# 64-column rows and 64x128 tiles for the turned sums of w, 40 weight columns for the turned state

## The chip, the cores and the metric

The kernel runs on one core of a Trainium2 chip. Its time is the device time of one execution in microseconds (us). Engines are named as in the profile: PE is TensorE's matmul, PEld its weight load, DVE is VectorE, ACT is ScalarE, POOL is GpSimd, and SP issues the DMAs.

## The reference

A recurrent attention layer (RWKV-7) over 4 batches, 8 heads, 768 positions and 40 columns a head, all FP32, and a two-layer network with exact GELU on its output:

```python
for t in range(S):
    y[:, :, t] = np.einsum('bhd,bhde->bhe', rt, state)
    Sa = np.einsum('bhde,bhe->bhd', state, at)
    state_decay = state * wt[:, :, None, :] - np.einsum('bhd,bhe->bhde', Sa, bt)
    state = state_decay + np.einsum('bhd,bhe->bhde', vt, kt)
...
x = attn_out.transpose(0, 2, 1, 3).reshape(B * S, H * D)     # 3072 x 320
h = x @ w_in                                                 # 320 x 2048
g = 0.5 * h * (1.0 + erf(h / sqrt(2)))
return g @ w_out                                             # 2048 x 320
```

## The kernel before

The 768 positions are cut into 12 chunks of 64 (`C`). Within a chunk the recurrence is turned into matrix products: with the running products of w (as exponentials of running sums of its logarithms) taken into a, r, b and k, a chunk needs products of 64x64, one inverse of a triangular matrix for each batch and head, and the state from the chunk before. The 128 partitions hold two halves of 64 (`half(0)`, `half(1)`); a head's 40 columns or rows stand in 64 places of a half.

Each piece of the work is a step, a generator named by its kind and its chunk (`w0` loads w of chunk 0, `sums0` sums its logarithms). A list written out by hand, `ORDER`, says in which order the steps go on; a number behind a colon names the pair of PSUM banks (`duo`) that a piece takes. Every engine carries out its instructions in the order in which the list issues them, and waits only for the data it needs. All loads of a step go into SP's queue, except stored inverses, which POOL issues. The list opens with `tails0 gaps1 w0 pads3 consts0 w1 pads2 zeros1 inv1 b0 a0 logs0 begin6`, and goes on to `sums0:0 sums0:1 v0 k0 logs1 sums0 wi0 consts0 sums1:2 sums1:3 pads0 ta0:1 sums0 pads1 sc0 sums1 ta0 tb0:0`. The change leaves it as it is.

The steps that matter here:

- `w` loads w of a chunk with positions on partitions. Chunks 0 and 2 go into `w_tile`, chunk 1 into the tile `SM`, which later holds masked sums; a row of a batch has its 8 heads side by side, 40 columns each. Behind the last head lie 24 columns (`REST`), zeroed by POOL in `tails`, since a matmul that takes 64 columns from the last head's start reads them.
- `logs` takes the logarithm in place (ACT, line 514).
- `sums` of the first three chunks has two parts. First the turned sums: for each head and each half of the positions one matmul with 64 columns of w's logarithms as weights (the head's 40 and 24 of the next one) and a triangular matrix of ones, `cum_m`, as the moving side; the running sums come out with a head's columns on partitions. Then the straight sums: one matmul for each batch pair with `cum_m` as weights and 320 moving columns. ACT takes the exponentials: those of the straight sums in place of w (line 537), the turned ones into `wpT` (line 540).
- `sc` (DVE, line 613) and `sk` (POOL, line 621) multiply b and k by the straight exponentials. In chunks 0 and 1 the products go into slices of the tile `extra`, called `padded`: slice `c % 2` for b, slice `2 + c % 2` for k. There each head has 64 columns, of which `pads` zeroes the last 24 (POOL, line 377); the list issues `pads3` and `pads2` near its start.
- `ta`, `tb`, `tk` turn a, b and k (PE, line 572); `N`, `A`, `RV` are products of 64x64; `sq`, `cornerd`, `joinedd` invert chunk 0's matrix on PE, `inv` the other chunks' on POOL (lines 819 and 821), through DRAM (`nb`, `ft`).
- `tn` turns the state for the products with r: 40 rows of `st` as weights, an identity of 40 columns as moving side. For chunks 1 and 2 it works on full 128 rows; from chunk 3 on there are 32 matmuls a chunk, each with 64 weight columns (the 40 of the state and the 24 next to them). ACT copies the result to the tile `turned` (line 1009), whose rows of each half up to 40 `yy` then uses as weights.
- `ph`, `pc`, `pd`, `pg`, `po` are the two-layer network (lines 1191 to 1347), which fills PE between the pieces of the recurrence.

One FP32 matmul stands in the trace as two records of PE and two of PEld. Most small matmuls go through the helper `mm` and so have its line, 154; they are told apart by their tiles and shapes, such as `64*128 64x128`: 64 rows and 128 columns of weights, then rows and columns of the moving side.

Of the kernel before, what the change touches and what calls it, by code (L numbers as in the profile page):

```python
# [13 lines left out]
ACT = mybir.ActivationFunctionType  # L14
# [83 lines left out]
def kernel(  # L98
# [15 lines left out]
    nc = tc.nc  # L114
    B, H, S, D = r.shape
    DM, DF = moe_w_in.shape
    P = 128
    C = 64
    HP = 64
    BL = 32  # L120
    NP = H // 2
    NA = H // 4
    G = B // 2
# [6 lines left out]
    REST = HP - D  # L130
# [7 lines left out]
    def sb(name, shape, dtype=FP32):  # L138
        return const.tile(shape, dtype, name=name)
# [4 lines left out]
    def duo():  # L144
        return duos[places.pop(0)]

    def half(j, n=HP):
        return slice(j * HP, j * HP + n)
# [4 lines left out]
    def mm(o, lhsT, rhs, first=True):  # L153
        nc.tensor.matmul(o, lhsT, rhs, start=first, stop=True, skip_group_check=True)  # L154
# [3 lines left out]
    NT, NB, NW, NS = FIRST  # L158
# [4 lines left out]
    w_tile = sb("w_tile", [P, G * DM + REST])  # L163
# [5 lines left out]
    b_rows, k_rows = ([t[:, n * RW:(n + 1) * RW] for t in two_rows] for n in range(2))  # L169
    st = sb("st", [P, 2, NP, G, VC])  # L170
    SM = sb("SM", [P, 2, G, NP, VC])
# [7 lines left out]
    TW = 2 * G * NP * D  # L179
    turned = sb("turned", [P, LW])  # L180
# [13 lines left out]
    def plain(t):  # L194
        return t.rearrange(" ".join(["p"] + list("abcd")[:len(t.shape) - 1]) + " -> p (" + " ".join("abcd"[:len(t.shape) - 1]) + ")") \
            if len(t.shape) > 2 else t

    padded = extra.rearrange("p (n g h d) -> p n g h d", n=4, g=G, h=H)
# [11 lines left out]
    raws, queue = {}, [nc.sync]  # L210

    def rows(t):
        return t[:, :G * DM].rearrange("p (g h d) -> p g h d", g=G, h=H)

    def rows_of(src, c, e):
        return src[G * e:G * (e + 1), :, c * C:(c + 1) * C, :].rearrange("g h t d -> t (g h) d")
# [4 lines left out]
    def load(out, in_):  # L221
        queue[0].dma_start(out=out, in_=in_)  # L222

    def fetch(c, n, src, t):
        for e in range(2):
            load(t[half(e)].rearrange("p g h d -> p (g h) d")[:, :, :D], rows_of(src, c, e))
        raws[c, n] = t
# [17 lines left out]

    @step
    def w_(c):
        t = plain(SM)[:, :G * DM + REST] if c == 1 else w_tile
        to = rows(t)
        if c < NB:  # L250
            fetch(c, "w", w, to)
            raws[c, "w"] = t
            yield
        else:
            for e in range(2):
                for g in range(G):
                    load(to[half(e ^ g), g], w[G * e + g, :, c * C:(c + 1) * C].rearrange("h t d -> t h d"))
                raws[c, "w"] = t
                yield
# [59 lines left out]
    ident = sb("ident", [P, P])  # L319
    cum_m = sb("cum_m", [P, P])  # L320
# [7 lines left out]

    @step
    def tails(c):  # L330
        for t in (w_tile, plain(SM)) if c == 0 else (b_rows[0], k_rows[0]):
            nc.gpsimd.memset(t[:, G * DM:G * DM + REST], 0.0)
        yield

# [173 lines left out]
    def of(c):  # L508
        return this.setdefault(c, {})

    @step
    def logs(c):
        logw = raws[c, "w"][:, :G * DM]
        nc.scalar.activation(logw, logw, ACT.Ln)
        yield

    @step
    def sums(c):
        t, logw = of(c), raws.pop((c, "w"))
        wp = t["wp"] = wps[c % 2]  # L520
        if c < NW:
            pt = duo().rearrange("p e (n t) -> p e n t", t=C)
            for n in range(G * NP):
                for x in range(2):
                    for e in range(2):
                        at = (2 * n + x) * D
                        mm(pt[half(x), e, n], logw[half(e), at:at + HP], cum_m[half(e), half(e)])
            yield
        cum = duo()[:, :, :DM]
        for g in range(G):  # L530
            for e in range(1 if c < NB else 2):
                q = half(e ^ g) if c >= NB else slice(0, P)
                mm(cum[half(e) if c >= NB else q, g], cum_m[q, q], logw[q, g * DM:(g + 1) * DM])
        yield
        rw = logw[:, :G * DM].rearrange("p (g m) -> p g m", g=G)
        t["rw"] = rows(logw)
        nc.scalar.activation(rw, cum, ACT.Exp, scale=-1.0)  # L537
        yield
        if c < NB:
            nc.scalar.activation(wp[:, :, 1:].rearrange("p (n e) t -> p e n t", e=2), pt, ACT.Exp)  # L540
            yield
        elif c < NW:
            en = t["en"] = by_batch(kT_tile)
            for to, scale_ in ((wp[:, :, 1:].rearrange("p (g n e) t -> p g e n t", g=G, e=2), 1.0),
                               (en.rearrange("p (e g n) t -> p g e n t", e=2, g=G), -1.0)):
                for g in range(G):
                    nc.scalar.activation(to[:, g], pt[:, ::1 - 2 * g, g * NP:(g + 1) * NP], ACT.Exp, scale=scale_)
            yield
# [37 lines left out]
    def by_batch(t):  # L586
        return t.rearrange("p g n t -> p (g n t)").rearrange("p (n t) -> p n t", t=C)
# [402 lines left out]
    @step  # L990
    def tn(c):
        if c < NB:
            pt = duo()[:, :, :NP * BW].rearrange("p e (n t) -> p e n t", n=NP)
            for e in range(2):
                for i in range(NP):
                    for g in range(G):
                        mm(pt[half(g), e, i], st[:, e, i, g, :HP], ident.rearrange("p (x d) -> p x d", x=2)[:, :, :D])
            yield
            nc.scalar.copy(turned[:, :TW].rearrange("p (e n) -> p e n", e=2), pt.rearrange("p e n t -> p e (n t)"))
            yield  # L1000
            return
        pt = duo()[:, :, :G * NP * D].rearrange("p x (n d) -> p x n d", d=D)
        for e in range(2):
            for i in range(NP):
                for g in range(G):
                    for x in range(2):
                        mm(pt[half(g), x, e * NP + i], st[half(x, D), e, i, g, :HP], ident[half(x, D), half(x, D)])
        yield
        nc.scalar.copy(turned[:, :TW].rearrange("p (n x d) -> p x n d", x=2, d=D), pt)
        yield  # L1010

    def sums_of_y(c):
# [424 lines left out]
```

## Time and profile before

| What | us |
|---|---|
| median of 3 runs | 660.76 |
| lowest and highest run | 656.54, 661.46 |
| span of the profiled execution, first to last instruction | 653.2 |
| PE busy | 633.2 (97%) |
| PEld busy | 573.0 (88%) |
| DVE, ACT, POOL busy | 483.1, 274.7, 387.0 |

The profile page gives no time of its own for the profiled execution but its span; the time of a run holds what lies around the span too, 3.3 us by the lowest run and 8.3 us by the highest. The share of busy time is an average over stages: the first 130 us load the weights and bring the first chunks in, with DMA near its limit, and the last 100 us have little but the network left.

### The profile page before, as it was taken

To read this page: it belongs to the slowest core of one execution; us is meant where nothing else is said; L and a number is where in the kernel's file an instruction comes from. 1 tells how busy PE (TensorE), PEld (TensorE's weight loads), DVE (VectorE), ACT (ScalarE), POOL (GpSimd) and SP (SyncE) were. 2 spreads that over 40 slices of the span, in tenths; PEclk is the share of its full clock that TensorE was granted. 3 is DMA by queue.
4 is the path that set the end of the run, shared out by engine and by line. 5 is a ranking of instruction groups with operands and counts; after the bars stand their busy time and mean duration, and the time that the engine had idled before them with its cause. 6 is when DMAs were issued, how large, how long until landed. Compare 5 with 4: busy or idle time off the path is not lost.

```text
span 653.2 us, 31493 instructions
## 1 busy us (share of the span) xinstructions
PE 633.2 (97%) x14128; PEld 573.0 (88%) x14128; DVE 483.1 (74%) x643; ACT 274.7 (42%) x327; POOL 387.0 (59%) x797
## 2 busy tenths in 40 slices
PE   9998999989999999999999999999999999999997
PEld 5887788766888989999989989999999998998987
DVE  1697999997687997875976988886895874834442
ACT  4365574553334333515534345444433445135130
POOL 5258624865857865846857856868834877811000
PEclk9999999999999999999999999999999999999999
DMA  9999989568576776877776767696577865330100
GB/s 128 167 173 182 192 182 177 134 148 148 106 141 118 137 129 123 150 141 114 141 145 116 134 115 146 126 162 129 111 132 146 134 125 96 60 71 5 31 12 21
DMA packets 299111, 80.76 MB, mean 124 GB/s; under 512 B 287688, under 2 KB 292560, under 8 KB 298976
## 3 DMA queue, kind: packets, MB, share of 16 engines
q1 hardware_dynamic: 297872, 76.23, 63.5%
q0 software_dynamic: 864, 2.36, 2.1%
q8 instruction: 110, 1.80, 1.2%
q14 instruction: 25, 0.20, 0.1%
q10 hardware_dynamic: 240, 0.16, 0.1%
HBM read 65.40 MB, written 11.01 MB: 117 GB/s over the span
## 4 chain that ended last, share of the span: by engine, by line
PE 65%; POOL 10%; DMA 8%; SPq 6%; DVE 5%; issue 4%; ACT 2%; DVEq 0%; POOLq 0%; ACTq 0%
PE duo L154 25%; PE duo L1310 15%; PE duo L1216 10%; PE duo L1191 6%; SPq L222 6%; POOL tmp L819 5%; POOL W L821 5%; PE duo L1294 4%; PE duo L1223 3%; PE duo L572 2%; DMA Tt<-inv 2%; DMA inv<-W 2%; DMA Nb<-N 1%; DMA rows<-in_k_dram 1%; DMA inv<-rT 1%
## 5 line engine op out<-in xcount | busy, mean ns | idle before, releaser
L819 POOL TENSOR_TENSOR tmp<-W,Nb 128x56 f32<-128x56 f32 (+22 forms) x155 | 77.5, 500 | 60.5 <-DMA Nb<-N 48.7
L1310 PE MATMUL duo<-w_out_sb,gt 128*128 128x160 f32 x640 | 93.2, 302 | 1.9 <-ACT gt L1268 1.2
L819 POOL TENSOR_TENSOR tmp<-rT,Nb 128x56 f32<-128x56 f32 (+22 forms) x155 | 71.3, 460 | 35.7 <-DMA Nb<-N 23.9
L1310 PEld LDWEIGHTS duo<-w_out_sb,gt 128*128 128x128 f32 x640 | 87.7, 190 | 5.0 <-ACT gt L1268 1.4
L821 POOL TENSOR_TENSOR W<-W,tmp 128x56 f32<-128x56 f32 (+22 forms) x155 | 77.2, 498 | 12.1
L821 POOL TENSOR_TENSOR rT<-rT,tmp 128x56 f32<-128x56 f32 (+22 forms) x155 | 74.1, 478 | 12.1
L1216 PE MATMUL duo<-xt,w_in_sb 64*128 64x128 f32 x864 | 61.5, 275 | 0.0
L1254 ACT COPY gt<-duo 128x1024 f32<-128x1024 f32 x27 | 27.3, 1011 | 72.9 <-PE duo L1216 46.3
L1260 DVE TENSOR_TENSOR gt<-gt,duo 128x1024 f32<-128x1024 f32 x27 | 32.8, 1213 | 32.9 <-ACT gt L1254 17.3
L1223 PE MATMUL duo<-xt,w_in_sb 64*128 64x128 f32 x576 | 56.2, 272 | 0.0
L1191 PE MATMUL duo<-xt,w_in_sb 64*128 64x256 f32 x480 | 55.6, 382 | 0.6 <-ACT SM L962 0.4
L1216 PEld LDWEIGHTS duo<-xt,w_in_sb 64*128 64x128 f32 x864 | 54.1, 188 | 1.7 <-DVE spare L692 0.5
L1191 PEld LDWEIGHTS duo<-xt,w_in_sb 64*128 64x128 f32 x480 | 45.3, 187 | 7.6 <-ACT SM L962 0.8
L1310 PE MATMUL duo<-extra,conv 128*128 128x160 f32 x320 | 46.8, 302 | 0.5 <-issue 0.5
L1310 PEld LDWEIGHTS duo<-extra,conv 128*128 128x128 f32 x320 | 43.9, 190 | 1.6 <-issue 0.9
L1223 PEld LDWEIGHTS duo<-xt,w_in_sb 64*128 64x128 f32 x576 | 44.1, 188 | 0.0
L621 POOL TENSOR_TENSOR rows<-rows,w_tile 128x640 f32<-128x640 f32 x9 | 15.6, 1737 | 43.6 <-ACT w_tile L537 29.4
L1266 ACT ACTIVATE gt<-gt 128x1024 f32<-128x1024 f32 x27 | 28.2, 1056 | 29.3 <-DVE gt L1260 29.0
L1294 PE MATMUL duo<-w_out_sb,gt 128*128 128x320 f32 x128 | 37.0, 440 | 0.5 <-ACT w_tile L537 0.5
L1294 PEld LDWEIGHTS duo<-w_out_sb,gt 128*128 128x128 f32 x128 | 23.5, 190 | 10.2 <-ACT w_tile L537 0.6
L1314 DVE TENSOR_TENSOR os<-os,duo 128x160 f32<-128x160 f32 x40 | 12.7, 317 | 24.9 <-PE duo L1310 22.2
L962 ACT COPY SM<-duo 128x832 f32<-128x832 f32 (+1 forms) x22 | 17.4, 827 | 26.8 <-PE duo L154 26.8
(257 smaller groups left out, 1420.1 us busy)
## 6 DMA issues: line engine op xcount, KB each, us to landing
Nb<-N SPq DMA_DIRECT2D x18, 256.0 KB
VR<-in_v_dram SPq DMA_DIRECT2D x24, 160.0 KB
out_dram<-os SPq DMA_DIRECT2D x45, 80.0 KB
rows<-in_b_dram SPq DMA_DIRECT2D x22, 160.0 KB
rows<-in_k_dram SPq DMA_DIRECT2D x22, 160.0 KB
w_out_sb<-in_moe_w_out_dram SPq DMA_DIRECT2D x5, 640.0 KB
w_tile<-in_w_dram SPq DMA_DIRECT2D x36, 80.0 KB
Tt<-inv SPq DMA_DIRECT2D x44, 64.0 KB
```

The lines of the kernel that those rows point to most:

```text
L154: nc.tensor.matmul(o, lhsT, rhs, start=first, stop=True, skip_group_check=True)
L222: queue[0].dma_start(out=out, in_=in_)
L819: eng.tensor_tensor(t, W[:, :nr, j:j + 1].to_broadcast([P, nr, rest]), Nb[:, j:j + 1, j + 1:].to_broadcast([P, nr, rest]), ALU.mult)
L821: eng.tensor_tensor(W[:, :nr, j + 1:], W[:, :nr, j + 1:], t, ALU.add)
L1191: nc.tensor.matmul(pt[:, x, s], w_in_sb[half(x), kt, p * P:(p + 1) * P], xt[half(x), kt], start=kt == 0, stop=kt == NK - 1)
L1216: nc.tensor.matmul(out_of(pt)[:, x, j], left(kt, j)[half(x)], right[half(x), kt], start=first and j == 0 and kt == 0, stop=True, skip_grou ...
L1223: nc.tensor.matmul(out_of(pt)[:, x, j], w_in_sb[half(x), NP, at:at + P], xt[half(x), NP, cols], start=False, stop=True, skip_group_check=True)
L1254: nc.scalar.copy(block_of(f, g), out_of(of(c)["u"]))
L1260: nc.vector.tensor_tensor(block_of(f, g), block_of(f, g), out_of(of(c)[v_]), ALU.add)
L1266: nc.scalar.activation(block_of(f, g), block_of(f, g), ACT.Gelu)
L1294: nc.tensor.matmul(pt[:, g], gt[:, f, g * P:(g + 1) * P], w_out_sb[:, f], start=f == 0, stop=f == NF - 1)
L1310: nc.tensor.matmul(pt[:, n, :DM // 2], l_[:, f], r_[:, f], start=f == 0, stop=f == NF // 2 - 1)
```

## The change

The rows of w of chunks 0 and 1 are loaded into `padded[:, 2]` and `padded[:, 3]`, 64 columns a head, where logarithms, exponentials and, at the end, k's products replace each other in place. Two heads are 128 neighbouring columns there, with zeros in the gaps, so one matmul with 128 weight columns takes the place of two with 64: `sums0` and `sums1` issue 16 matmuls for the turned sums instead of 32. The straight sums read the 40 columns of each head with a stride. `w_tile` serves chunk 2 and later ones alone, and `SM` its masked sums alone. `tn` from chunk 3 on takes 40 weight columns instead of 64, and ACT copies 104 partitions instead of 128.

```diff
@@ w_
-        t = plain(SM)[:, :G * DM + REST] if c == 1 else w_tile
+        t = w_tile
         to = rows(t)
-        if c < NB:
+        if c < 2:
+            fetch(c, "w", w, padded[:, 2 + c])
+            yield
+        elif c < NB:
             fetch(c, "w", w, to)
             raws[c, "w"] = t
             yield
@@ tails
-        for t in (w_tile, plain(SM)) if c == 0 else (b_rows[0], k_rows[0]):
+        for t in (w_tile,) if c == 0 else (b_rows[0], k_rows[0]):
@@ logs
-        logw = raws[c, "w"][:, :G * DM]
+        logw = raws[c, "w"][:, :, :, :D] if c < 2 else raws[c, "w"][:, :G * DM]
@@ sums
-            for n in range(G * NP):
-                for x in range(2):
+            if c < 2:
+                by_heads = logw.rearrange("p g h d -> p (g h d)")
+                for n in range(G * NP):
                     for e in range(2):
-                        at = (2 * n + x) * D
-                        mm(pt[half(x), e, n], logw[half(e), at:at + HP], cum_m[half(e), half(e)])
+                        mm(pt[:, e, n], by_heads[half(e), n * P:(n + 1) * P], cum_m[half(e), half(e)])
+            else:
...
-                mm(cum[half(e) if c >= NB else q, g], cum_m[q, q], logw[q, g * DM:(g + 1) * DM])
-        yield
-        rw = logw[:, :G * DM].rearrange("p (g m) -> p g m", g=G)
-        t["rw"] = rows(logw)
-        nc.scalar.activation(rw, cum, ACT.Exp, scale=-1.0)
+                mm(cum[half(e) if c >= NB else q, g], cum_m[q, q],
+                   logw[:, g, :, :D] if c < 2 else logw[q, g * DM:(g + 1) * DM])
+        yield
+        rw = t["rw"] = logw[:, :, :, :D] if c < 2 else rows(logw)
+        nc.scalar.activation(rw, cum.rearrange("p g (h d) -> p g h d", d=D), ACT.Exp, scale=-1.0)
@@ tn
-                        mm(pt[half(g), x, e * NP + i], st[half(x, D), e, i, g, :HP], ident[half(x, D), half(x, D)])
-        yield
-        nc.scalar.copy(turned[:, :TW].rearrange("p (n x d) -> p x n d", x=2, d=D), pt)
+                        mm(pt[half(g, D), x, e * NP + i], st[half(x, D), e, i, g, :D], ident[half(x, D), half(x, D)])
+        yield
+        nc.scalar.copy(turned[:HP + D, :TW].rearrange("p (n x d) -> p x n d", x=2, d=D), pt[:HP + D])
```

More of the change, by code (lines that the diff above doesn't have):

```diff
@@ L522, in sums @@
             pt = duo().rearrange("p e (n t) -> p e n t", t=C)
-            for n in range(G * NP):
-                for x in range(2):
+            if c < 2:
+                by_heads = logw.rearrange("p g h d -> p (g h d)")
+                for n in range(G * NP):
                     for e in range(2):
-                        at = (2 * n + x) * D
-                        mm(pt[half(x), e, n], logw[half(e), at:at + HP], cum_m[half(e), half(e)])
+                        mm(pt[:, e, n], by_heads[half(e), n * P:(n + 1) * P], cum_m[half(e), half(e)])
+            else:
+                for n in range(G * NP):
+                    for x in range(2):
+                        for e in range(2):
+                            at = (2 * n + x) * D
+                            mm(pt[half(x), e, n], logw[half(e), at:at + HP], cum_m[half(e), half(e)])
             yield
```

## The prediction

> **What bounds the kernel now.** I read the page's busy shares and the chain first, then the busy time by stretches, then the start and one turned state in order of time, then the groups of matmuls by shape. The page:
>
> ```profile
> PE 633.2 (97%) x14128; PEld 573.0 (88%) x14128; DVE 483.1 (74%) x643; ACT 274.7 (42%) x327; POOL 387.0 (59%) x797
> PE 65%; POOL 10%; DMA 8%; SPq 6%; DVE 5%; issue 4%; ACT 2%; DVEq 0%; POOLq 0%; ACTq 0%
> ```
>
> PE carries two thirds of the chain that ended last, and POOL with its DMAs nearly a fifth. By stretches (busy us of PE, PEld, DVE, ACT, POOL, then the granted clock, the DMA share and GB/s):
>
> ```profile
> 8.50:13.40 4.90, 4.90 (x138) 3.51 (x138) 0.14 (x1) 2.16 (x3) 1.51 (x3) 1.00 1.32 148
> 17.00:59.20 42.20, 41.24 (x1072) 36.48 (x1071) 32.81 (x56) 23.15 (x33) 21.53 (x44) 1.00 0.94 179
> 59.20:62.30 3.10, 0.06 (x5) 0.01 (x2) 3.07 (x5) 0.72 (x1) 2.77 (x5) 1.00 0.56 84
> 62.30:67.00 4.70, 4.70 (x91) 3.33 (x93) 4.70 (x10) 0.53 (x1) 4.01 (x9) 0.64 1.12 156
> 67.00:112.00 45.00, 44.15 (x1112) 37.99 (x1108) 42.67 (x76) 26.70 (x37) 18.47 (x47) 1.00 0.91 188
> 377.00:450.00 73.00, 72.14 (x1728) 67.96 (x1731) 57.50 (x70) 32.85 (x37) 50.93 (x104) 1.00 0.74 135
> 480.00:544.00 64.00, 62.80 (x1480) 59.82 (x1470) 44.77 (x55) 25.62 (x30) 38.90 (x81) 1.00 0.70 125
> ```
>
> From 8.5 to 112 us PE hardly rests but for one hole of 3 us at 59.2: what is added to PE at the start moves all that follows. From 377 to 450 and from 480 to 544 PE is as full (98%), but the chain goes by POOL's inverses there (below), so PE time saved in those two stretches turns into idle time.
>
> **Part one, the sums of w.** The start, in order of time:
>
> ```profile
> 4.70 0.42 POOL L377 MEMSET extra<- 128x384 f32 x1
> ...
> 5.56 1.28 ACT L514 ACT_TABLE_LOAD   x1 [5.56 <-DMA w_tile<-in_w_dram]
> ...
> 6.86 0.74 ACT L514 ACTIVATE w_tile<-w_tile 128x640 f32<-128x640 f32 x1
> ...
> 8.71 1.16 PE L154 MATMUL duo<-cum_m,w_tile 64*64 64x64 f32 x64
> ...
> 9.80 1.34 PE L154 MATMUL duo<-w_tile,cum_m 128*128 128x320 f32 x4
> ...
> 11.07 1.16 PE L154 MATMUL duo<-cum_m,SM 64*64 64x64 f32 x64
> ...
> 11.22 1.28 ACT L537 ACT_TABLE_LOAD   x1 [2.91 <-PE duo L154]
> ...
> 16.97 1.16 PE L154 MATMUL duo<-aT,nT 40*64 40x64 f32 x64
> ```
>
> Each FP32 matmul stands as two records, so the 32 small matmuls of `sums0` are 64. From their first start to the next group's they take 9.80 - 8.71 = 1.09 us, 17 ns a record, four tiles at a time. After the change there are 32 records of 64x128 tiles for each chunk, two tiles at a time, still with 64 moving columns. Is the pace set by the records, by the moving columns or by the weight columns? These groups tell (busy us, mean ns):
>
> ```profile
> L154 PE MATMUL duo<-w_in_sb,Nb 64*64 64x64 f32 x64 | 2.2, 221 | 0.0
> L154 PE MATMUL duo<-w_in_sb,Nb 64*64 64x32 f32 x64 | 2.0, 218 | 0.0
> ```
>
> and these starts, later in the run:
>
> ```profile
> 205.10 0.75 PE L154 MATMUL duo<-Tt,Js 32*32 32x32 f32 x64
> 205.78 2.43 PE L1191 MATMUL duo<-xt,w_in_sb 64*128 64x256 f32 x20
> ...
> 250.09 2.06 PE L1216 MATMUL duo<-xt,conv 64*128 64x128 f32 x32
> 252.08 1.66 PE L154 MATMUL duo<-SM,Tt 64*64 64x104 f32 x64
> ```
>
> With 64 weight columns, half the moving columns took 2.0 us instead of 2.2: the weights set the pace. 32 records with 128 weight columns on 64 rows took 252.08 - 250.09 = 1.99 us. Those also moved 128 columns, so 1.99 us is the upper bound of the new group; if the records alone counted, 32 would take half of 1.09, 0.55 us, the lower bound. I take 1.9, near the upper end, because of the 64x32 row. That is 1.9 - 1.09 = +0.8 us for each of two chunks, **+1.6 us** (bounds -0.5 to +0.9 each). PE's order puts both groups ahead of everything else of chunk 0, with `ta0`, `tb0` and `N0` behind them. Chunk 0's group delays ACT's table load and the exponentials by 0.8, chunk 1's delays the two transposes by 1.6; the DVE scaling between them then waits for less than PE does. No slack follows before 59 us, so 1.6 stays.
>
> The rest of part one I cost at nothing. The Ln of chunk 0 ends at 7.60, a microsecond before PE is free of its first matmuls at 8.7, which covers a load that lands somewhat later in 64-column rows. The zeros of those rows are written by POOL at 4.70 to 5.12, ahead of the new reader; were this memset to wait for the load of the same rows, POOL would be held to 5.6, where ACT starts, and the cover of 3 us would still do. One memset of 24 columns less is 0.12 us on POOL, which is not the bound here. The strided operands: DVE and POOL
>
> ```profile
> L613 DVE SCALAR_TENSOR_TENSOR rows<-rows,w_tile x9: 782/819/827, 152.2 to 595.1; 128x640 f32<-128x640 f32 x9
> L613 DVE SCALAR_TENSOR_TENSOR extra<-xt,SM x1: 818/818/818, 15.7 to 15.7; 128x640 f32<-128x640 f32 x1
> L621 POOL TENSOR_TENSOR extra<-rT,SM x1: 1555/1555/1555, 39.7 to 39.7; 128x640 f32<-128x640 f32 x1
> ```
>
> take 818 ns with a 64-column output and 819 without, so I expect the same of an input. Two tiles come free earlier, and nobody waits for them:
>
> ```profile
> 24.91 1.54 POOL L621 TENSOR_TENSOR extra<-rows,w_tile 128x640 f32<-128x640 f32 x1 [14.90 <-DMA rows<-in_k_dram]
> ...
> 40.95 2.17 SPq L222 DMA_DIRECT2D w_tile<-in_w_dram  x2
> ...
> 54.03 2.08 DVE L977 TENSOR_TENSOR SM<-duo,left_upper 128x416 f32<-128x416 f32 x4
> ```
>
> SP issues w of chunk 2 at 40.95, 14 us after the last reader of chunk 0's sums ended; SM is overwritten at 54.03, 13 us after POOL's product for chunk 1. `k` now replaces the sums in place, and its reader is the same as before.
>
> **Part two, the turned state.** `tn` of chunks 3 to 11, nine times 64 records:
>
> ```profile
> 176.09 1.14 PE L154 MATMUL duo<-ident,st 40*64 40x40 f32 x64
> 177.04 1.64 PE L154 MATMUL duo<-VR,nT 64*64 64x104 f32 x64
> ```
>
> It takes 0.95 us now; the group of 32 weight columns above takes 205.78 - 205.10 = 0.68. In a straight line 40 columns make 0.68 + 0.27 x 8/32 = 0.75, so -0.20 us; bounds 0 (if the array loads 64 columns anyway) and -0.27. ACT's copy of 104 instead of 128 partitions has as many columns and keeps its time. Which of the nine lie on the chain (chain in order of time, first and last of the six that do, then the three that don't):
>
> ```profile
> 176.16 3.45 PE duo L154 x192
> ...
> 264.67 3.58 DMA VR<-in_v_dram
> ...
> 411.81 1.38 POOL tmp L819
> ...
> 512.55 1.33 POOL W L821
> ...
> 566.21 2.02 PE duo L154 x128
> ```
>
> At 266, 415 and 513 us the chain is with a load or with POOL, and the saving is lost; the other six give 6 x 0.20 = **-1.2 us** (bounds 0 and 9 x -0.27 = -2.4).
>
> The Trainium skill, "TensorE: Matmul & The Clock Gate", section "LDWEIGHTS (loading the stationary operand)", puts a weight load at its columns divided by 1.2 in ns, whatever the rows. By it a round of tiles goes from 53 to 107 ns in the sums and from 53 to 33 in the turned state; with 16 rounds each my estimate from that page would be +1.7 and -1.9 on the path, -0.2 in all. The rows above agree in direction.
>
> **The sum.** +1.6 - 1.2 = +0.4 us. The profiled execution's span is 653.2 us; the runs are 656.54 to 661.46, so 3.3 to 8.3 us lie around it, and neither part touches those. Against the median of 660.76 this gives 661.2 us: no change that can be told, since about 1% (6.6 us) is what a measurement of this kernel can tell from none.
>
> **The rivals.**
>
> A. The turned state gains nothing: 40 columns are loaded as 64, as the array's shapes here are 32, 64 or 128 wide, or the instructions come no faster. For it:
>
> ```profile
> PEld duo L154 <- issue: 22.2, 66, 3.2
> q8 instruction: 110, 1.80, 1.2%
> ```
>
> The weight loads of these small matmuls waited 22.2 us for nothing that the profile shows, and 2 x 14128 records in 110 instruction packets are 257 for a packet: a quick group eats its packet sooner. Against it: the 32-column group did run faster. 660.76 + 1.6 = 662.4.
>
> B. The records set the pace, not the weight columns. Then 32 records less save 0.5 us for each chunk (1.09 / 2), and 40 columns save nothing: 660.76 - 1.0 = 659.8. Against it: 17 ns a record in `sums0`, 0.68/64 = 11 ns in the 32-column group and 62 in the 128-column one. The Trainium skill, in the same page's section "Wait — 56ns, not 53.3ns?", gives a floor of about 25 ns between starts however small the matmul; the trace's 11 ns across tiles is below it, so here the measurement decides.
>
> C. **Slower.** Behind the sums every packet of instructions is cut at another place, 128 records later in the program (32 matmul and 32 weight-load records less in each chunk). Two holes of this kind in the chain, the longest last:
>
> ```profile
> 43.55 0.45 issue
> ...
> 59.25 3.04 issue
> ```
>
> The second cost 3.04 us, and the clock of 0.64 in the 4.7 us behind it cost 4.7 x 0.36 = 1.7 more, 4.7 together, while DMA was 94% busy ahead of it. If the new cuts fall so that one more packet comes late by over 3 us in the loaded first 130 us, the time is 661.2 + 4.7 = 665.9; from two such holes on, 670.6, it is slower by over 1%. Against it: up to 59 us the next longest is the first, 0.45 us.
>
> D. The same cut the other way: the hole at 59 us closes and the clock stays up, 661.2 - 4.7 = 656.5, which is also the fastest run before.
>
> **How the numbers follow.** Forecast 0.52 (alone 659.8 to 662.6: +1.4 to +1.8 for the sums, 0 to -2.4 for the turned state), A 0.17, B 0.09, C 0.12, D 0.10. Runs of the same kernel differ by 4.9 us, as much as C and D. The range from 655.5 to 666.5 takes in D, the forecast's bounds, A, B and C with one hole; it leaves C with more holes and D with another gain out, under 2 in 10. Faster by over 1% (below 654.2) needs D and more: 0.04. Slower by over 1% (above 667.4) is the far part of C: 0.08. Within: 0.88.
>
> **What would show it.** Right: the sums' groups of 32 records take 1.8 to 2.0 us each from start to next start, `N0` starts near 18.6 instead of 16.97, the turned states take 0.70 to 0.80 us instead of 0.95. Wrong in part one: the groups take about 1.0. Wrong in part two: `tn` still takes 0.95 with 40 weight columns. C or D: the idle time under "issue" grows or falls by 3 us, and the granted clock near 62 us says which. A wait of ACT's Ln, of POOL's pad memsets or of SP's loads that is new in the first 20 us would show that I overlooked an order of the tiles.

## The result and the profile after

| | median us | runs | span of the profiled execution |
|---|---|---|---|
| before, the three runs above and one more beside it | 659.84 | 656.54 to 661.46 (4) | 653.2 |
| after | 678.07 | 675.10 to 682.22 (4) | 680.5 |

The change made the kernel slower: the ratio is 1.0293, 95% interval 1.0241 to 1.0345. The forecast was 661.2 us and its range ended at 666.5. The profiled execution is a run of 682.22 us, so 1.7 us lie around its span, and 1.7 to 3.4 us do in the other runs whose span is on record: the 3.3 to 8.3 us given for the kernel before set a span beside the times of other runs. Its profiled execution, with a span of 653.2 us, was one of the quick ones, while 682.22 us is the slowest run of the changed kernel. The two profiles are therefore 27.3 us apart, and the medians 18.2.

The page of the changed kernel, the lines that answer to those of before:

```profile
PE 645.6 (95%) x14064; PEld 584.6 (86%) x14064; DVE 481.9 (71%) x643; ACT 275.0 (40%) x327; POOL 377.3 (55%) x796
PE 83%; DVE 8%; issue 5%; DMA 1%; ACT 1%; SPq 1%; DVEq 0%; ACTq 0%
q8 instruction: 110, 1.80, 1.2%
```

PE has 64 matmul records fewer and is busy 12.4 us longer. POOL has left the chain, PE's share rose from 65% to 83%: a kernel that was bound by PE in two thirds of its chain is now bound by it in five sixths. Nothing new is computed, so PE's own time must have grown. Two views say how. First the mean granted clock of the execution, before and then after:

```profile
core 0: 653.2 us, clock 0.997
```

```profile
core 0: 680.5 us, clock 0.979
```

Time lost to the lower clock: (1 - 0.997) x 653.2 = 2.0 us before, (1 - 0.979) x 680.5 = 14.3 after, **12.3 more**. Then the waits of PE and PEld that no event of the trace ends (total us, times, longest), before:

```profile
PEld duo L154 <- issue: 22.2, 66, 3.2
PE duo L154 <- issue: 5.4, 6, 3.0
```

and after:

```profile
PEld duo L154 <- issue: 39.5, 78, 3.5
PE duo L154 <- issue: 20.4, 14, 3.4
```

On line 154 PE stands still for **15.0 us more** (20.4 - 5.4), in 14 holes instead of 6. The span's growth splits by PE's busy time as well: busy 12.4 us longer (645.6 - 633.2), not busy 14.9 us longer (680.5 - 645.6 = 34.9 against 20.0), 27.3 together. The clock's 12.3 us are of the size of the first part, the holes' 15.0 of the size of the second. The match is not exact. The same view has further rows of PE's "issue" on other lines (3.3 us after, 0.7 before), some of PE's other waits became shorter, and 1.2 us of the clock's loss fall into holes. But the sizes leave little for anything else. The holes are spread over the whole run (chain in order of time, pieces of "issue" in which PE stands still):

```profile
49.42 1.13 issue
66.62 2.59 issue
88.75 2.15 issue
...
185.80 1.96 issue
225.23 1.02 issue
235.34 1.51 issue
260.03 2.09 issue
...
534.15 3.39 issue
571.32 1.45 issue
```

Behind the longest the clock is down. By stretches, the hole and what follows it:

```profile
534.10:537.60 3.50, 0.11 (x6) 0.06 (x4) 0.73 (x1) 1.95 (x4) 2.98 (x7) 0.73 1.39 164
537.60:543.00 5.40, 5.40 (x54) 5.11 (x54) 3.00 (x3) 0.00 (x0) 4.66 (x10) 0.54 0.53 100
```

The last three columns are the granted clock, the DMA share and GB/s. The trace's record of the clock has six such stretches in the changed kernel before PE's last work, each at 0.50 of full speed, four of 3.41 us and two of 6.83; they begin behind the holes at 49.42, 88.75, 260.03 and 571.32, and inside those at 367.57 and 534.15. Other holes, of up to 2.59 us, have none. The kernel before has one, behind its hole at 59.25. The Trainium skill ("TensorE: Matmul & The Clock Gate", section "What's actually happening") says that an idle PE falls back to half its clock and needs about 3.4 us of work to get out; the trace agrees with both, with 0.50 and with 3.41 us or twice that.

### The profile page after: what moved, and what is told of

The parts are those of the page before. It is cut to its first block, busy times and chain, and to the rows that moved or that the text cites. A ratio compares the mean times of both kernels' runs of the same rounds, so it can differ in the third digit from the quotient of the medians.

```text
span 680.5 us, 31363 instructions
## 1 busy us (share of the span) xinstructions
PE 645.6 (95%) x14064; PEld 584.6 (86%) x14064; DVE 481.9 (71%) x643; ACT 275.0 (40%) x327; POOL 377.3 (55%) x796
## 4 chain that ended last, share of the span: by engine, by line
PE 83%; DVE 8%; issue 5%; DMA 1%; ACT 1%; SPq 1%; DVEq 0%; ACTq 0%
PE duo L154 28%; PE duo L1319 22%; PE duo L1225 17%; PE duo L1200 6%; PE duo L1232 5%; PE duo L1303 4%; PE duo L581 1%; SPq L222 1%; DVE conv L490 1%; DMA a_pairs<-in_a_dram 1%; DVE conv L484 1%; DVE conv L586 1%; DVE conv L568 0%; DMA rows<-in_k_dram 0%; DVE conv L475 0%
## 5 line engine op out<-in xcount | busy, mean ns | idle before, releaser
L828 POOL TENSOR_TENSOR tmp<-W,Nb 128x56 f32<-128x56 f32 (+22 forms) x155 | 75.0, 484 | 60.4 <-DMA Nb<-N 48.6
L830 POOL TENSOR_TENSOR rT<-rT,tmp 128x56 f32<-128x56 f32 (+22 forms) x155 | 68.0, 438 | 12.2
L1225 PE MATMUL duo<-xt,w_in_sb 64*128 64x128 f32 x864 | 61.7, 275 | 0.0
L1200 PE MATMUL duo<-xt,w_in_sb 64*128 64x256 f32 x480 | 57.5, 391 | 3.0 <-issue 2.1
L1232 PE MATMUL duo<-xt,w_in_sb 64*128 64x128 f32 x576 | 58.6, 279 | 0.9 <-issue 0.9
L1263 ACT COPY gt<-duo 128x1024 f32<-128x1024 f32 x27 | 27.3, 1011 | 74.1 <-PE duo L1225 45.7
L1200 PEld LDWEIGHTS duo<-xt,w_in_sb 64*128 64x128 f32 x480 | 47.4, 191 | 9.9 <-issue 2.8
L1225 PEld LDWEIGHTS duo<-xt,w_in_sb 64*128 64x128 f32 x864 | 54.2, 188 | 1.8 <-DVE spare L701 0.5
L1319 PE MATMUL duo<-extra,conv 128*128 128x160 f32 x320 | 48.2, 309 | 0.0
L1232 PEld LDWEIGHTS duo<-xt,w_in_sb 64*128 64x128 f32 x576 | 46.3, 195 | 1.0 <-issue 1.0
L1319 PEld LDWEIGHTS duo<-extra,conv 128*128 128x128 f32 x320 | 45.7, 196 | 0.8
L996 DVE TENSOR_TENSOR SM<-duo,left_upper 128x832 f32<-128x832 f32 (+1 forms) x22 | 20.8, 990 | 12.2 <-PE duo L154 12.0
```

The source lines that it names most:

```text
L828: eng.tensor_tensor(t, W[:, :nr, j:j + 1].to_broadcast([P, nr, rest]), Nb[:, j:j + 1, j + 1:].to_broadcast([P, nr, rest]), ALU.mult)
L830: eng.tensor_tensor(W[:, :nr, j + 1:], W[:, :nr, j + 1:], t, ALU.add)
L996: nc.vector.tensor_tensor(sm_of[:, x, :, :, wanted(c)], pt[x][:, :, :, wanted(c)], mask, ALU.mult)
L1200: nc.tensor.matmul(pt[:, x, s], w_in_sb[half(x), kt, p * P:(p + 1) * P], xt[half(x), kt], start=kt == 0, stop=kt == NK - 1)
L1225: nc.tensor.matmul(out_of(pt)[:, x, j], left(kt, j)[half(x)], right[half(x), kt], start=first and j == 0 and kt == 0, stop=True, skip_grou ...
L1232: nc.tensor.matmul(out_of(pt)[:, x, j], w_in_sb[half(x), NP, at:at + P], xt[half(x), NP, cols], start=False, stop=True, skip_group_check=True)
```

## Where the holes sit

Count PE's records from hole to hole (same view, PE's and PEld's counts in the brackets), in the changed kernel:

```profile
50.53:69.20 18.67, 16.07 (x381) 12.59 (x382) 15.45 (x25) 10.62 (x14) 16.32 (x31) 0.91 1.02 189
69.20:90.88 21.68, 19.34 (x510) 16.75 (x510) 20.73 (x34) 9.52 (x13) 12.87 (x32) 1.00 0.90 184
226.23:236.82 10.59, 9.09 (x256) 8.34 (x256) 9.10 (x12) 4.91 (x6) 9.34 (x17) 1.00 0.73 124
236.82:262.10 25.28, 23.19 (x511) 22.18 (x510) 20.41 (x26) 7.22 (x9) 10.60 (x26) 1.00 0.74 129
```

763, 1020, 512 and 1021: but for a few records, multiples of 256, which is what 2 x 14064 records over 110 instruction packets of 1.80 MB in all make: 256 instructions of 64 bytes each. The few that are missing are instructions that the view does not count, 96 for semaphores and 3 others. Numbered with them, all 17 of PE's waits for "issue" in this trace (those over 0.15 us, on every line) end at record 193 or 194 of a count of 256, and so do all 136 in the 14 traces of this case. The trace also has the transfers of the packets, 110 of 16384 bytes: PE goes on 1.25 to 1.98 us after the end of one in each of the 17 waits, and over all 14 traces never sooner than 1.17 us. So a hole stands where a packet ends and the next has not come.

Which packets come late? The transfer of the next one begins, in the median, 1.1 us after PE has crossed into the present one, and takes 0.88 to 1.65 us. PE's work in a packet, its holes left out, is 5.5 us in the median of the changed kernel, and 14 of the 17 waits stand behind packets of only 1.8 to 3.2 us, in which two or three groups of small matmuls meet. The stretch behind the turned state of chunk 3 in the changed kernel, PE alone:

```profile
182.95 0.83 PE L154 MATMUL duo<-ident,st 40*40 40x40 f32 x64
183.61 1.66 PE L154 MATMUL duo<-VR,nT 64*64 64x104 f32 x64
185.05 0.74 PE L154 MATMUL duo<-rT,turned 40*64 40x64 f32 x35
187.76 0.68 PE L154 MATMUL duo<-rT,turned 40*64 40x64 f32 x29 [1.96 <-issue]
```

The cut falls in the middle of the third group, 35 records into it, and PE waits 1.96 us. In the kernel before, the same third group ran through:

```profile
178.50 1.11 PE L154 MATMUL duo<-rT,turned 40*64 40x64 f32 x64
179.54 2.42 PE L1294 MATMUL duo<-w_out_sb,gt 128*128 128x320 f32 x8
```

The change took 64 records (32 matmul, 32 weight load) out of each of chunks 0 and 1, 128 in all: half a packet. Every later cut moved by half a packet. Of the 109 whole packets in each of the two traces, 13 held less than 4 us of PE's work before, and 26 do after.

## The experiments

The theory, called P: the loss is the place of the packets' cuts. Rivals: R, the faster turned state asks for instructions faster than they come; W, PE's delay at the start makes it collide with the loads. The ratio is to the kernel before, run beside each, with its 95% interval; it took 657.81, 655.37 and 657.01 us in the three sessions, so ratios compare across them and medians do not, and the first expectations in us, made beside the 659.84 above, lie some 2 us high.

**One part at a time.** `tn_only` has the diff's lines in `tn` alone, `sums_only` all its other lines.

> The kernel before with part two alone (40 weight columns in the turned state); no instruction is added or removed. Theory P (packets): PE's instructions come in packets of 256, and the change lost its time because 128 PE instructions fewer at the start cut the packets at other places, so that quick groups share a packet and PE waits for the next one. By P this kernel keeps its cuts and gains the 0.27 us of each turned state that are on the path: 657 to 660 us, idle time of PE under issue about 5 us as before. Rival R (rate): the quicker turned state asks for the next packet sooner, and the holes behind it (four of the changed kernel's are in the product with r just behind it) are its own; by R 668 to 678.

> Part one alone (64-column rows and 64x128 tiles for w of chunks 0 and 1), the turned state with 64 columns as before. By P all of the loss: 673 to 681 us, with idle time of PE under issue above 15 us and several drops of the granted clock. By R only the two groups' cost: 661 to 663. Rival W (time): the 1.7 us that PE is late at the start make its packets collide with the loads; W gives 670 to 680 here as P does, and is told apart by the next two kernels.

`tn_only` took 656.38 us, ratio 0.9986 (0.9955 to 1.0018); `sums_only` 676.60 us, ratio 1.0297 (1.0244 to 1.0350). The loss is all in the part that removes instructions. R falls. PE's idle time on line 154 under "issue" is 7.3 us in the first (about 5 were expected) and 18.1 in the second.

**The number of instructions alone.** In nine kernels the last two of the six large matmuls at the start, which keep PE at work while it waits for the first logarithms, give way to small ones, here 32 + 2:

```diff
@@ begin
-        for n in range(c):
+        for n in range(c - 2):
             mm(pt[:, n % 2], w_in_sb[:, 0, :P], w_in_sb[:, 0, :512])
+        for n in range(32 + 2):
+            mm(pt[half(n % 2), n // 2 % 2, :HP], w_in_sb[half(n // 2 % 2), 0, :HP], w_in_sb[half(n // 2 % 2), 0, :HP])
         yield
```

Two of the 34 stand for the two removed, 32 add 4 instructions each, 128.

> The changed kernel with 32 small matmuls (64 columns by 64, results unused) in the place of the last two of the six large ones that keep PE warm at the start: 128 PE instructions more, about 1 us of PE time in a stage where PE waits for the logarithms. The cuts lie as before the change. By P 659 to 663 us. By W and R, to which the number of instructions is nothing, 675 to 681.

> The kernel before with the same 32 small matmuls: nothing of the change, but every later cut of PE's packets 128 instructions earlier in the program, where 256 is a packet (so the cuts lie as in the changed kernel). By P 670 to 680 us. By R and W 659 to 662.

The changed kernel with 128 instructions more: 656.04 us, ratio 0.9974 (0.9944 to 1.0004), below the 659 to 663 expected. The whole loss is gone. The kernel before with 128 more, and nothing of the change: 675.98 us, ratio 1.0280 (1.0208 to 1.0351). The whole loss is there. Its trace has the hole at the very same record, 35 into the product behind the turned state, although its turned state is the old one:

```profile
175.79 1.14 PE L154 MATMUL duo<-ident,st 40*64 40x40 f32 x64
176.75 1.64 PE L154 MATMUL duo<-VR,nT 64*64 64x104 f32 x64
178.21 0.74 PE L154 MATMUL duo<-rT,turned 40*64 40x64 f32 x35
180.23 0.69 PE L154 MATMUL duo<-rT,turned 40*64 40x64 f32 x29 [1.28 <-issue]
```

and the padded changed kernel has none there, with the fast turned state:

```profile
178.41 0.83 PE L154 MATMUL duo<-ident,st 40*40 40x40 f32 x64
179.07 1.66 PE L154 MATMUL duo<-VR,nT 64*64 64x104 f32 x64
180.52 1.14 PE L154 MATMUL duo<-rT,turned 40*64 40x64 f32 x64
```

PE's waits of this kind: 17.6 us in the kernel before with 128 more, 3.5 us in the changed one with 128 more. Packets with less than 4 us of work: 26 in the first and 13 in the second, as in the changed kernel and the kernel before.

```profile
PE duo L154 <- issue: 17.6, 14, 3.1
```

```profile
PE duo L154 <- issue: 3.5, 3, 1.5
```

W falls with these two. The padded changed kernel starts `N0` at 19.01 us, the changed one at 19.30, and it is fast; the padded kernel before starts it at 16.29, earlier than the 16.97 of the kernel before, and it is slow.

**A whole packet, and none.** The same diff with 64 + 2 small matmuls (256 instructions more) and with 0 + 2 (as many as before).

> 64 small matmuls at the start are 256 PE instructions, a whole packet: the cuts lie where they lie in the kernel before, one packet later in count. By P 0.999 to 1.006 (the start itself may lose 2 to 3 us to a hole at its first crossing, as the kernel with 48 did, 2.0 us at 11 us). If it is the number of added instructions that counts, or their being small, worse than the kernel with 32: above 1.028.

> The control of the filler: the kernel before with the last two of the six large matmuls at the start replaced by two small ones, as many instructions as before. By P 0.998 to 1.002. If the missing large matmuls themselves cost time (a clock that comes up later), 1.003 to 1.010, and the 0.6% of the kernel with 12 small ones would be theirs.

659.27 us, ratio 1.0037 (1.0006 to 1.0068), and 658.06 us, ratio 1.0021 (0.9993 to 1.0048). Twice the instructions that cost 2.8% cost 0.4%: what counts is the number modulo 256. The filler itself costs 0.2% by the medians, between nothing and 0.5% by the interval, and half of the 0.4% may be its own.

**Other places of the cut.** 48 + 2 and 12 + 2 small matmuls in the kernel before, 12 + 2 with part two, 24 + 2 in the changed kernel (its cuts 32 instructions later in the program than before the change).

> The kernel before with 48 small matmuls at the start, 192 PE instructions more: the cuts lie 192 earlier in the program. Theory P with an estimate from the trace of before (each packet of 256 instructions needs 4.0 to 4.6 us from the crossing of the one before, and what the work in it falls short of that is a hole): the holes add up to 4.5 to 7.8 us at the cuts of before, 9 to 18 with 128 instructions more, 10 to 18 with 192, 1 to 4 with 48. So here 667 to 678 us. If it is not where the cuts lie but that half a packet is missing, 658 to 665.

> The kernel before with 12 small matmuls at the start, 48 PE instructions more, which by the same estimate is where the cuts cost least (1 to 4 us of holes instead of 4.5 to 7.8). By P 652 to 656 us. If cuts matter only when they move by about half a packet, as before: 657 to 659.

> The same 12 small matmuls and part two of the change (40 weight columns in the turned state), a version that may beat both kernels: by P 650 to 655 us, the gain of the cuts and that of part two (1 to 2 us) together.

> The changed kernel with 24 small matmuls: cuts 32 instructions later in the program than in the kernel before. Between the place of before (1.00) and that of the change (1.029, 128 later): by the estimate of holes 5 to 9 us there against 4.5 to 7.8, so 0.998 to 1.008; a version that may come out fastest if the best cut lies on that side.

| cut, against the kernel before | kernel | median us | ratio | 95% interval |
|---|---|---|---|---|
| 192 instructions earlier | before, 48 + 2 | 663.29 | 1.0127 | 1.0098 to 1.0155 |
| 128 earlier | before, 32 + 2 | 675.98 | 1.0280 | 1.0208 to 1.0351 |
| 48 earlier | before, 12 + 2 | 659.08 | 1.0059 | 1.0030 to 1.0088 |
| 48 earlier | part two, 12 + 2 | 658.09 | 1.0063 | 1.0038 to 1.0087 |
| the same | after, 32 + 2 | 656.04 | 0.9974 | 0.9944 to 1.0004 |
| 32 later | after, 24 + 2 | 663.24 | 1.0085 | 1.0058 to 1.0113 |
| 128 later | after | 678.07 | 1.0293 | 1.0241 to 1.0345 |

My estimate of holes had the order of the far places right and the best place wrong: 48 earlier should have been the fastest and is 0.6% slower, 192 earlier was put at 667 us or more and took 663, inside the 658 to 665 of its rival, and 32 later came out just above what I gave. The version meant to beat both kernels was put at 650 to 655 us and took 658. What speaks against the rivals of these runs, by which only half a packet counts, is that 192 earlier, 48 earlier and 32 later have intervals that lie above 1.00, though 0.2% of each may be the filler's. It took the same 4.0 to 4.6 us for every packet, and the packets' times are not the same: the next transfer begins anywhere from 2.2 us before to 4.2 us after the crossing in the changed kernel. So the time cannot be foretold to half a per cent from one trace in this way. Of the places tried, that of the kernel before is the fastest by the medians; I did not find a version that is surely faster than it.

**The rows and the tiles, with the cut held.** `rows_only` keeps 32 matmuls of 64 weight columns on the 64-column rows:

```diff
@@ sums (c < 2)
-                        mm(pt[:, e, n], by_heads[half(e), n * P:(n + 1) * P], cum_m[half(e), half(e)])
+                        for x in range(2):
+                            mm(pt[half(x), e, n], by_heads[half(e), n * P + x * HP:n * P + (x + 1) * HP], cum_m[half(e), half(e)])
```

with the old `tn`. `sums_pad32` is part one with 32 + 2 small matmuls at the start.

> The 64-column rows of w alone: chunks 0 and 1 lie in the padded slices, but their turned sums keep 32 matmuls of 64 columns each, and the turned state is as before. The number and order of PE's instructions are those of before. By P (packets) the rows cost nothing: ratio 0.998 to 1.003. If the place of w or the freed tiles matter: off by more than 0.5%.

> Part one alone with 32 small matmuls at the start, so that its cuts lie as in the kernel before: what the wider tiles cost without their cuts. By the prediction's term +1.6 us: 659 to 661 beside about 658. If PE had slack behind the start, 657 to 659.

659.33 us, ratio 1.0020 (0.9993 to 1.0048), and 655.78 us, ratio 1.0018 (0.9992 to 1.0043). The rows cost nothing that can be told. Part one with its cut put back may cost up to 2.8 us (0.43% of 655.4) or gain half a microsecond; the 1.6 us of the forecast are inside, and not shown.

## Why the prediction was wrong, point by point

**The groups of the sums: right.** The changed kernel's start:

```profile
9.42 2.00 PE L154 MATMUL duo<-cum_m,extra 64*128 64x64 f32 x32
11.35 1.34 PE L154 MATMUL duo<-extra,cum_m 128*128 128x320 f32 x4
...
19.30 1.16 PE L154 MATMUL duo<-aT,nT 40*64 40x64 f32 x64
```

The group takes 11.35 - 9.42 = 1.93 us; I had taken 1.9. The weight columns set its pace. `N0` starts 2.33 us later than before, of which 0.71 is a start at 9.42 instead of 8.71 (the granted clock came up at 6.67 us instead of 5.24, so more of the large matmuls in front ran under the lower clock) and 1.62 what follows, nearly all of it the two groups; I had 1.6.

**The turned state: right in kind, with a larger gain than forecast.** The groups of chunk 8, before and then after:

```profile
415.25 1.09 PE L154 MATMUL duo<-ident,st 40*64 40x40 f32 x64
416.27 2.44 PE L1310 MATMUL duo<-w_out_sb,gt 128*128 128x160 f32 x16
```

```profile
433.79 0.81 PE L154 MATMUL duo<-ident,st 40*40 40x40 f32 x64
434.54 2.44 PE L1319 MATMUL duo<-w_out_sb,gt 128*128 128x160 f32 x16
```

0.75 us instead of 1.02; where the next group is of small matmuls too it is 183.61 - 182.95 = 0.66 instead of 0.95. So a turned state gains 0.27 to 0.29 us, and not 0.20: the forecast drew its line between a group of 32 columns with long matmuls behind it (0.68) and one of 64 with small ones behind it (0.95). With long ones behind both, 0.68 and 1.02, the line gives 0.77 for 40 columns, and the three such groups took 0.75 to 0.81. The weight load of 40 columns is not rounded up to 64, so A is out, and with both groups B is too. On the whole kernel the saving of 1.2 us fits `tn_only`, and cannot be told from nothing.

**The step that failed is C.** I had the mechanism, packets cut 128 records away, and its price for one hole with the clock behind it, 4.7 us. I had it wrong in its extent: the sum put the moved cuts at nothing, and C and D made of them one hole more or less in the first 130 us, with chances of 0.12 and 0.10 that nearly balanced; only 0.08 was left for everything above 667.4 us. But a moved cut moves all 110 packets, over the whole run. The groups of the recurrence have 64 matmul records, which is 128 instructions and just half a packet, so two or three of them can meet in one. Whether they do depends on where they stand, and they stand everywhere (the eleven products with `turned` of the kernel before start at places from 2 to 236 of their packets). At its old place 13 packets held less than 4 us of work, 128 records later 26. So this is a count over all packets and no single draw, and one that could be made from the trace of before. Two rows pointed at it. The weight loads waited 22.2 us for "issue" in 66 places, beside a single hole of 3 us. And "the next longest is 0.45 us" held up to 59 us only: the same trace has a hole of 0.54 us at 73.04 and one of 0.89 at 330.49, far from the loaded start. That the kernel before, whose order was written by hand, has one of the better places was not known; why it has is open. What the runs put in the place of the term: +15.0 us of holes and +12.3 us of clock in the profiled execution, 18.2 us in the medians, not 4.7 us with a small chance.

**What the fetch hides.** The Trainium skill ("Runtime: NRT & Kernel Launch", section "Instruction fetch mechanics") says that an engine's instructions are fetched in blocks of 256 while the present one runs, and that the cost of crossing a block is mostly hidden. The block size agrees with the counts above. The hiding does not hold here: 20.4 us of PE's waits in the changed kernel. By that rule the forecast of 661 us would have stood.

**What else was costed at nothing** holds, with one small sign that I overlooked: ACT's logarithm of chunk 1 waits 0.38 us for its load, which it did not before. It ends at 8.88 us, ahead of the matmuls of chunk 1 at 12.62, and costs nothing. `rows_only` bounds the 64-column rows, the freed tiles and the strided operands together at +0.5%.

## What to carry to other kernels

When PE is bound by many short matmuls, the count of its instructions ahead of a stretch is a parameter of that stretch: divide PE's records, matmuls and weight loads, by instruction packets, look for waits under "issue" that lie a whole number of packets apart, and ask of every edit that adds or removes PE instructions where it moves the cuts. An edit's own cost can be measured only with the cuts held, by as many filler instructions as it removed, put where PE waits anyway; here part one read as +3.0% without them and as +0.2% with them. Count the work in each packet at the old and at the new cuts: here twice as many short packets went with a loss of 2.9%, and putting the cuts back took it away.

## What the runs showed of the hardware

With long matmuls behind them, 64 records of small matmuls took 0.68 us with 32 weight columns, 0.75 to 0.81 with 40, and 1.02 with 64. 256 instructions more at the start cost 0.4%, 128 cost 2.8%. PE's instructions came in packets of 256, and no packet was begun sooner than 1.17 us after its transfer had ended. A hole of 3.39 us in PE's work was followed by 5.4 us at a mean clock of 0.54; over the changed kernel's profiled execution the clock lost 12.3 us more than before beside 15.0 us more of holes, so that late packets cost PE nearly twice their lateness in sum, though not each of them lowered the clock.
